# Sixteen unread identity products in TensorE's line ahead of the first inverse

## The chip, the cores and the metric

One Trainium2 chip, one of its cores. The metric is the device time of one launch in microseconds. Between executions of the same kernel it varies: three timed runs of the kernel before gave 660.37, 661.7 and 666.66 us.

## The reference

The inputs are r, k, v, w, a, b of shape (4, 8, 768, 40), that is batch, heads, sequence, head size, and the weights of a gated projection behind it. First a recurrence with a 40 x 40 state for each batch and head:

```python
for t in range(S):
    y[:, :, t] = np.einsum('bhd,bhde->bhe', rt, state)
    Sa = np.einsum('bhde,bhe->bhd', state, at)
    state_decay = state * wt[:, :, None, :] - np.einsum('bhd,bhe->bhde', Sa, bt)
    state = state_decay + np.einsum('bhd,bhe->bhde', vt, kt)
```

Then y, laid out as x of shape (4, 768, 320), goes through the second part:

```python
h = np.maximum(x @ w_in, 0.0)                 # 320 -> 1024
u, v = h[..., :512], h[..., 512:]
v_n = (v - mean(v)) / np.sqrt(var(v) + 1e-06) # over the last axis
v_s = np.einsum('ts,bsd->btd', w_spatial, v_n) + b_spatial[None, :, None]
return (u * v_s) @ w_out                      # 512 -> 320
```

## The kernel before

`tile_kernel` (line 36) runs `phase1` (217), which does the recurrence and the first product up to u and the normalised v, and then `phase2` (102), which does the product over time, the gate and the last product.

**Chunks and steps.** The recurrence is taken in chunks of C = 64 tokens: 12 chunks for each of two pairs of batches, together NS = 24 steps. A step handles 16 batch-and-head states at once: NU = 8 units, each with two heads on the two halves of the 128 partitions. Within a chunk the sequential rule becomes linear algebra: products of the decayed inputs, a triangular system that is solved with an inverse of 64 x 64 blocks, and an update of the state Mc that the next step reads.

**The inversion.** Four steps (GS = 4) share one inversion. `lprime` (325) and `lblock` (340) make the 32 x 32 triangular blocks of a step, `invert` (347) then inverts those of four steps together by forward substitution on VectorE: a transpose into A (351), then 30 pairs of a multiply into the PSUM tile itmp (362) and an add from it (366), each pair on the result of the pair ahead, and two transposes of the result, XT0 (371) and X11 (373). The inversions of the later groups are spread over the steps ahead of their use; the first, `invert(0)`, is issued whole ahead of the steps (line 916), since step 0 needs it.

**Step by step on TensorE.** `c_bp` (526) multiplies the state with the chunk's inputs; `c_ff` (544) takes the block products; `b_zt` (467) and `b_x21` (494) finish the 64 x 64 inverse from XT0 and X11 and the coupling block l21 of `b_l21` (449); `c_xx` (561) applies the inverse; `c_mp` (583) makes the next state, which `c_mp_out` (601, VectorE, line 607) scales; `c_y` (612) and `c_y_out` (623, VectorE, line 631) make the output y. `b_lka` (393), `b_h` (417) and `b_tok` (434, transposes by the identity `ident`) prepare the step behind. ScalarE copies results out of PSUM, GpSimd cuts triangles (`strict`, 404).

**What sets the order.** Each engine has its own line and runs it in order. Within `with tc.manual_schedule()` (863) that order is written by hand: `at(t, fn, ...)` puts a piece of work on a plan, where the whole part of t is the step and the fraction its place in it, and the plan is sorted and issued in that order. Work whose time is 24 or more, and phase 2, is issued outside that block, where a planner with a simulated timeline sets the order. For step 0 these entries bear on the change:

```python
FIRST = dict(REG, tok=0.37, tok_out=0.375, l21=0.45, l21_out=0.452, zt=0.47, zt_out=0.50, x=0.70,
             h=0.80, h_out=0.81, x21=0.65, x21_out=0.71)
at(T["tok"] + dt * par, b_tok, q, par)          # dt = 0.03
at(T["tok_out"] + dt * par, b_tok_out, q, par)
at(0.42, b_zt, 0)
at(0.43, b_xcopy, 0, act_copy)
at(0.44, b_zt_out, 0)
```

So in TensorE's line of step 0 stand `c_bp(0)` (0.00 and 0.05), `b_lka(1)` (0.115), `c_ff(0)` (0.30 and 0.35), `b_tok(1)` (0.37 and 0.40), `b_zt(0)` (0.42), which reads XT0 and so waits for the first inversion, `b_l21(1)` (0.45), `b_x21(0)` (0.455), `b_zt(1)` (0.47) and `c_xx(0)` (0.55 and 0.60).

**PSUM.** Pools ps_k, ps_c, ps_b, ps_i (the tile itmp) and ps_m (the tile pv, 128 x 512, one buffer). pv and itmp are used by the products of x with w_in (`m_ps`, 678; `m_v` 681 with 512 columns, `m_u` 728 with 256), which begin with step 11. Those are fp32r; the products of the recurrence are f32. `ident` is a 128 x 128 f32 identity, made at line 876.

Of the kernel before, what the change touches and what calls it, by code (L numbers as in the profile page):

```python
# [8 lines left out]
F32 = mybir.dt.float32  # L9
# [9 lines left out]
P = 128  # L19
# [12 lines left out]
DH = 512  # L32
# [184 lines left out]
def phase1(ctx, tc, early, late, vtok, win, xs, vns, uts, dscr):  # L217
    nc = tc.nc
# [7 lines left out]
    def pool(name, bufs=1, **kw):  # L226
        return ctx.enter_context(tc.tile_pool(name=name, bufs=bufs, **kw))
# [15 lines left out]
    ps_m = pool("ps_m", 1, space=PSUM)  # L243
# [11 lines left out]
    ident = const.tile([P, P], F32, name="ident")  # L255
# [7 lines left out]
    st, marks = {}, {}  # L263


    def prep_load(s, rows, cols=slice(0, EW), i=None, queues=(nc.sync, nc.sync)):
        t = ein[s % 2 if i is None else i]
        for par in range(2):
            o = par * 64
            queues[par].dma_start(out=t[o:o + rows, cols], in_=early[par, s, 0:rows, cols])  # L270
# [6 lines left out]
    def scan1(s, i=None):  # L277
        t = ein[s % 2 if i is None else i]
        Et = etp.tile([P, WF], F32, name="Et")
        at = fifo[s % 8].tile([P, NU, C], F32, name="at")  # L280
        sl = fifo[s % 8].tile([P, NU, 2, C], F32, name="sl")
        wseg = t[:, 0:WF]
        oth = t[:, WF:].rearrange("p (q n c) -> p n q c", q=3, c=C)
        sx = pin.tile([P, WF], F32, name="S", bufs=2)
        sv = sx.rearrange("p (n c) -> p n c", c=WSEG)
        st["pre", s] = (Et, at, sl)
        st["raw", s] = (wseg, oth, sv)
        nc.vector.tensor_tensor_scan(
            out=sx[:, ::-1], data0=wseg[:, ::-1], data1=ends[:, ::-1],
            initial=0.0, op0=ALU.mult, op1=ALU.add,  # L290
        )
        nc.vector.reciprocal(out=eseg[:, :, 0:1], in_=sv[:, :, 1:2])

    def scan2(s):
        Et, at, sl = st["pre", s]
        wseg, oth, sv = st["raw", s]
        nc.vector.tensor_tensor_scan(
            out=Et, data0=wseg, data1=ends, initial=0.0, op0=ALU.mult, op1=ALU.add,
        )

    def scr_store(s):
        if s % CPB == 0:
            return
        sv = st["raw", s][2]
        sc = jit.tile([P, NU], F32, name="sc")
        nc.scalar.activation(sc, sv[:, :, 1], AF.Copy)
        for par in range(2):
            nc.sync.dma_start(out=scr[s, par], in_=sc[RR[par]])

    def at_mul(s, eng, ns=slice(0, NU)):  # L310
        Et, at, sl = st["pre", s]
        oth = st["raw", s][1]
        Ev = Et.rearrange("p (n c) -> p n c", c=WSEG)
        eng.tensor_tensor(out=at[:, ns], in0=oth[:, ns, 0], in1=Ev[:, ns, 0:C], op=ALU.mult)

    def sl_mul(s, eng, ns=slice(0, NU)):
        Et, at, sl = st["pre", s]
        wseg, oth, sv = st["raw", s]
        k = ns.stop - ns.start
        eng.tensor_tensor(  # L320
            out=sl[:, ns], in0=oth[:, ns, 1:],
            in1=sv[:, ns, 2:C + 2].unsqueeze(2).broadcast_to([P, k, 2, C]), op=ALU.mult,
        )

    def lprime(s, units=range(NU)):
        Et, at, sl = st["pre", s]
        if units[0] == 0:
            st["pl", s] = ps_k.tile([P, NU, HB], F32, name="bk")
        pl = st["pl", s]
        for n in units:  # L330
            for blk in range(2):
                for par in range(2):
                    o = (1 - par) * 64 + blk * HB
                    cs = slice(blk * HB, (blk + 1) * HB)
                    nc.tensor.matmul(  # L335
                        pl[o:o + HB, n, :], lhsT=sl[PR[par], n, par, cs], rhs=at[PR[par], n, cs],
                        start=True, stop=True,
                    )

    def lblock(s):  # L340
        if s % GS == 0:
            st["Lc", s // GS] = inv.tile([P, GS * NU, HB], F32, name="Lc")
        Lc = st["Lc", s // GS]
        u0 = (s % GS) * NU
        nc.scalar.activation(Lc[:, u0:u0 + NU, :], st.pop(("pl", s)), AF.Copy, scale=-1.0)
# [33 lines left out]
    def lin_load(s, par):  # L379
        nc.sync.dma_start(out=lin[s % 2][RR[par], :, 0:LATE], in_=late[par, s])  # L380

    def vtok_load(s, par):
        nc.sync.dma_start(out=Rts[s % 2][par][PR[1 - par], :, C:], in_=vtok[s, par])
# [26 lines left out]
    def b_lka_out(s, par):  # L410
        At = st["blk", s][0]
        pk = st["pk", s]
        ev = PR[1 - par]
        nc.scalar.activation(At[par][ev], pk[ev], AF.Copy)  # L414
        strict(At[par][ev], NU)
# [97 lines left out]
    def grp(g):  # L513
        return slice(g * NP, (g + 1) * NP), range(g * NP, (g + 1) * NP)
# [229 lines left out]
    def at(t, fn, *args):  # L744
        plan.append((t, len(plan), fn, args))

    def step(gen):
        next(gen, None)

    v, p = nc.vector, nc.gpsimd  # L750

    def act_copy(out, in_):
# [4 lines left out]


    M1, M2, M3, M4 = 0.22, 0.46, 0.65, 0.80
    for s in range(NS):  # L760
        at(s + 0.02, scn_load, s)
        for g in range(NB):
            at(s + 0.00 + 0.05 * g, c_bp, s, g)
            at(s + 0.04 + 0.05 * g, c_bp_out, s, g)
            at(s + 0.30 + 0.05 * g, c_ff, s, g)
            at(s + 0.34 + 0.05 * g, c_ff_out, s, g)
            at(s + 0.55 + 0.05 * g, c_xx, s, g)
            at(s + 0.60 + 0.05 * g, c_xx_out, s, g)
            at(s + 0.74 + 0.02 * g, c_mp, s, g)
            at(s + 0.755 + 0.02 * g, c_mp_out, s, g)  # L770
            at(s + 0.86 + 0.04 * g, c_y, s, g)
            at(s + 0.90 + 0.04 * g, c_y_out, s, g)
            at(s + 0.95 + 0.01 * g, y_store, s, g)
# [34 lines left out]
    for q in range(GS, NS):  # L808
        t = PREP.get(q, q - 8 + 0.01)
# [47 lines left out]
    def pads(eng, t):  # L857
        w = t[:, 0:WF].rearrange("p (n c) -> p n c", c=WSEG)
        eng.memset(w[:, :, 1:C + 1], 1.0)
        eng.memset(w[:, :, 0:C + 2:C + 1], 0.0)  # L860
        eng.memset(t[:, WF:], 0.0)

    with tc.manual_schedule():
        W, O = slice(0, WF), slice(WF, EW)
        qs = (nc.sync, nc.scalar)
        nc.vector.memset(eseg[:, :, 0:C + 1], 0.0)
        nc.vector.memset(eseg[:, :, C + 1:], 1.0)
        pads(v, ein[1])
        pads(p, ein[2])
        pads(p, ein[3])  # L870
        for q, cols in ((0, W), (1, W), (0, O), (1, O), (2, W), (2, O), (3, W), (3, O)):
            prep_load(q, 48 if q else 64, cols, q, qs)
        for par in range(2):
            lin_load(0, par)
            vtok_load(0, par)
        make_identity(nc, ident)
        for t in (Mc, *xfs):
            p.memset(t, 0.0)
        for q in range(2):
            for rows in RR:  # L880
                diag = ident[rows, rows.start:rows.start + E]
                nc.scalar.activation(
                    lin[q][rows, :, LATE:], diag.unsqueeze(1).broadcast_to([E, NU, E]), AF.Copy
                )
        for q in range(2):
            scan1(q, q)
            scan2(q)
        for q in range(GS):
            if q > 1:
                scan1(q, q)  # L890
                scan2(q)
            scr_store(q)
            at_mul(q, v)
            for h in range(2):
                sl_mul(q, v, grp(h)[0])
                lprime(q, grp(h)[1])
            if q:
                lblock(q - 1)
        lblock(GS - 1)
        for par in range(2):  # L900
            b_copy(0, par)
        prep_load(4, 48)
        b_lka(0)
        for par in range(2):
            b_lka_out(0, par)
            b_tok(0, par)
            b_tok_out(0, par)
        b_l21(0)
        b_l21_out(0)
        b_h(0)  # L910
        for par in range(2):
            b_h_out(0, par)
            lin_load(1, par)
            vtok_load(1, par)
        prep_load(5, 48)
        for _ in invert(0):
            pass
        open_fifo()
        st["dec"] = late_bufs.enter_context(tc.tile_pool(name="dec", bufs=1))
# [3 lines that stand above are left out]
        at(0.455, b_x21, 0)  # L923
        at(0.46, b_x21_out, 0)
        plan.sort()
        n = 0
        while plan[n][0] < NS:
            t, _, fn, args = plan[n]
            fn(*args)
            n += 1  # L930
# [58 lines left out]
```

## Time and profile before

| | |
|---|---|
| timed runs, median (lowest to highest) | 661.7 us (660.37 to 666.66) |
| profiled execution, its own time | 664.58 us |
| its span, first to last instruction | 662.9 us |
| mean granted TensorE clock over the span | 0.941 |
| busy: TensorE, its weight loads, VectorE, ScalarE, GpSimd | 577.4, 523.0, 445.2, 394.3, 225.2 us |
| matmuls | 10960 |

The profile is of one execution on the chip. A row of a timeline has the start and length of a group of like instructions in us from the start of the span, the engine (PE is TensorE, PEld its weight loads, DVE VectorE, ACT ScalarE, POOL GpSimd), the line of the kernel, the operation, the tiles written and read, their shapes and the count; in brackets stands the idle time of the engine ahead of the group and what ended it. "Issue" is time in which an engine waited for nothing that the profile shows. The granted clock is the share of full speed that the throttle gave TensorE; in this profile it is either 1.0 or 0.5, and a figure between is a mean over a stretch. Matmuls are pipelined: the length of one is its own start to end, and the steps from start to start are shorter.

### The profile page before, as it was taken

What the parts mean: (1) busy time and instruction counts of PE and PEld (TensorE: products, weight loads), DVE (VectorE), ACT (ScalarE), POOL (GpSimd) and SP (SyncE); (2) the same over time, 40 slices, a digit from 0 to 9 for tenths busy, and PEclk for the clock granted to TensorE, in tenths of its full rate; (3) what the DMA queues carried; (4) which work ended last, traced back from release to release, by engine and by line L of the source; (5) the groups of instructions that cost most, each with busy time, mean ns of one, the idle gap of its engine ahead of it and who ended that gap; (6) DMA issues with size and microseconds to landing.
All of it is one profiled execution on the core that took longest, in us unless ns stands there. A gap on an engine that the chain in (4) does not pass through costs nothing.

```text
span 662.9 us, 25888 instructions
## 1 busy us (share of the span) xinstructions
PE 577.4 (87%) x10960; PEld 523.0 (79%) x10960; DVE 445.2 (67%) x951; ACT 394.3 (59%) x884; POOL 225.2 (34%) x312
## 2 busy tenths in 40 slices
PE   1628876478788888999999999999999999999998
PEld 1527766367677777888888888888888999999997
DVE  8898559978999999689787666443375844322221
ACT  2226654358676777788878888888774643232112
POOL 3113213104323334352341342323344935352121
PEclk9977787869798889999999999999999999999999
DMA  8754866458574756656666356365386558150001
GB/s 201 125 101 65 137 140 128 91 123 137 125 160 120 147 111 141 133 141 147 158 179 179 82 144 172 83 168 164 100 238 196 170 165 250 49 169 31 31 30 60
DMA packets 106587, 87.68 MB, mean 132 GB/s; under 512 B 35752, under 2 KB 92328, under 8 KB 104552
## 3 DMA queue, kind: packets, MB, share of 16 engines
q1 hardware_dynamic: 105928, 84.31, 52.4%
q10 hardware_dynamic: 544, 1.72, 1.1%
q8 instruction: 86, 1.41, 1.0%
q14 instruction: 29, 0.24, 0.1%
HBM read 59.20 MB, written 20.50 MB: 120 GB/s over the span
## 4 chain that ended last, share of the span: by engine, by line
PE 67%; DVE 13%; issue 7%; ACT 5%; DMA 5%; SPq 2%; POOL 1%; DVEq 0%; ACTq 0%; POOLq 0%
PE po L199 6%; PE pv L736 6%; PE pv L689 6%; PE pg L179 5%; PE pg L181 5%; PE pg L180 5%; PE bp L532 5%; PE ch L550 4%; PE ch L568 4%; PE bk L422 3%; PE bk L438 3%; DVE itmp L362 3%; PE bk L398 3%; DMA ein<-in_early 3%; DVE A L366 2%
## 5 line engine op out<-in xcount | busy, mean ns | idle before, releaser
L405 POOL TENSOR_SCALAR_AFFINE_SELECT Rt<-Rt 64x512 f32<-64x512 f32 (+1 forms) x144 | 83.8, 583 | 149.1 <-ACT Rt L578 113.6
L405 POOL TENSOR_SCALAR_AFFINE_SELECT At<-At 64x512 f32<-64x512 f32 x48 | 40.3, 840 | 149.9 <-ACT At L414 137.5
L362 DVE TENSOR_TENSOR itmp<-A 128x30 f32<-128x30 f32 (+9 forms) x180 | 68.7, 382 | 3.5
L542 ACT ACTIVATE Rt<-bp 64x416 f32<-64x416 f32 x96 | 49.1, 512 | 35.0 <-PE bp L532 33.2
L179 PE MATMUL pg<-wsh,vh 128*128 128x384 f32 x192 | 64.5, 336 | 1.1 <-ACT vh L51 1.1
L183 DVE TENSOR_TENSOR g<-pg,bb 128x384 f32<-128x384 f32 x32 | 17.8, 556 | 70.6 <-PE pg L181 67.9
L180 PE MATMUL pg<-wsl,vh 128*128 128x384 f32 x192 | 64.4, 335 | 0.0
L366 DVE TENSOR_TENSOR A<-A,itmp 128x30 f32<-128x30 f32 (+9 forms) x180 | 59.1, 328 | 6.1
L181 PE MATMUL pg<-wsh,vl 128*128 128x384 f32 x192 | 63.1, 336 | 0.0
L532 PE MATMUL bp<-lin,Mc 40*64 40x104 f32 x768 | 47.7, 280 | 16.7 <-DVE y L631 14.2
L532 PEld LDWEIGHTS bp<-lin,Mc 40*64 40x64 f32 x768 | 40.9, 151 | 20.2 <-DVE y L631 17.1
L55 POOL TENSOR_TENSOR gl<-g,gh 128x384 fp32r<-128x384 f32 x32 | 33.7, 1056 | 57.5 <-ACT gh L51 57.5
L578 ACT ACTIVATE Rt<-ch 64x416 f32<-64x416 f32 x96 | 49.2, 512 | 5.1 <-PE ch L568 2.7
L550 PE MATMUL ch<-Rt,At 128*64 128x104 f32 x768 | 46.9, 281 | 3.4 <-issue 2.6
L51 ACT ACTIVATE gh<-g 128x384 fp32r<-128x384 f32 x32 | 16.7, 522 | 54.5 <-DVE g L184 54.5
L550 PEld LDWEIGHTS ch<-Rt,At 128*64 128x64 f32 x768 | 41.3, 155 | 7.5 <-issue 4.2
L335 PE MATMUL bk<-at,sl 64*32 64x32 f32 x1536 | 22.4, 208 | 28.1 <-DVE sl L320 15.9
L335 PEld LDWEIGHTS bk<-at,sl 64*32 64x32 f32 x1536 | 18.7, 119 | 31.4 <-issue 13.2
L568 PE MATMUL ch<-ffs,xf 64*64 64x104 f32 x768 | 43.2, 267 | 0.0
L55 POOL TENSOR_TENSOR vl<-raw,vh 128x512 fp32r<-128x512 f32 x24 | 31.7, 1333 | 29.4 <-ACT vh L51 27.3
L607 DVE TENSOR_TENSOR Mc<-ch,scn 104x160 f32<-104x160 f32 x44 | 18.6, 439 | 32.8 <-PE ch L596 26.2
L568 PEld LDWEIGHTS ch<-ffs,xf 64*64 64x64 f32 x768 | 38.3, 144 | 1.1
(128 smaller groups left out, 1508.7 us busy)
## 6 DMA issues: line engine op xcount, KB each, us to landing
ein<-in_early SPq DMA_DIRECT2D x108, 129.0 KB
lin<-in_late SPq DMA_DIRECT2D x48, 160.0 KB
At<-at SPq DMA_DIRECT2D x48, 128.0 KB
uts<-ur SPq DMA_DIRECT2D x48, 128.0 KB
vns<-vr SPq DMA_DIRECT2D x24, 256.0 KB
raw<-vns SPq DMA_DIRECT2D x24, 256.0 KB
ut<-uts SPq DMA_DIRECT2D x24, 256.0 KB
Rt<-in_vtok SPq DMA_DIRECT2D x48, 80.0 KB
```

The lines of the kernel that those rows point to most:

```text
L55: eng.tensor_tensor(out=lo, in0=x, in1=hi.bitcast(F32), op=ALU.subtract)
L179: nc.tensor.matmul(pg, lhsT=vh[:, dc], rhs=w_h, start=(i == 0), stop=False)
L180: nc.tensor.matmul(pg, lhsT=vh[:, dc], rhs=w_l, start=False, stop=False)
L181: nc.tensor.matmul(pg, lhsT=vl[:, dc], rhs=w_h, start=False, stop=(i == NT - 1))
L362: nc.vector.tensor_tensor(out=tp, in0=A[:, k + 1:, k:k + 1].broadcast_to([P, m, k]), in1=A[:, k:k + 1, 0:k].broadcast_to([P, m, k]), op=AL ...
L366: nc.vector.tensor_tensor(out=A[:, k + 1:, 0:k], in0=A[:, k + 1:, 0:k], in1=tp, op=ALU.add)
L405: nc.gpsimd.affine_select(out=t, in_=t, pattern=[[0, k], [1, C]], base=0, channel_multiplier=-1, compare_op=ALU.is_gt, fill=0.0,)
L532: nc.tensor.matmul(bp[PR[par], q, :], lhsT=Mc[RR[par], n, :], rhs=li[RR[par], n, C:], start=(q == 0), stop=False, skip_group_check=True,)
L542: nc.scalar.activation(Rt[par][PR[par], gp, :], st["bp", g][PR[par]], AF.Copy)
L550: nc.tensor.matmul(ff[PR[1 - par], q, :], lhsT=At[par][:, n, :], rhs=Rt[par][:, n, :], start=True, stop=True,)
L568: nc.tensor.matmul(xx[ev, q, :], lhsT=xf[ev, n, :], rhs=ffs[ev, q, :], start=True, stop=True,)
L578: done = nc.scalar.activation(Rt[par][PR[par], gp], xx[PR[1 - par]], AF.Copy, scale=-1.0)
```

## The change

A helper `beat(k)` issues k matmuls of the identity by itself: the stationary operand is `ident`, the moving one `ident` repeated four times (512 columns), the target a PSUM tile pv that is allocated from ps_m ahead of the hand-written block. Each starts and ends its own accumulation. Sixteen of them are put on the plan at 0.415 of step 0. Nothing reads what they write.

```diff
     def step(gen):
         next(gen, None)
 
+    def beat(k):
+        for _ in range(k):
+            nc.tensor.matmul(
+                st["beat"], lhsT=ident, rhs=ident.unsqueeze(1).broadcast_to([P, 4, P]), start=True, stop=True
+            )
+
     v, p = nc.vector, nc.gpsimd
...
     M1, M2, M3, M4 = 0.22, 0.46, 0.65, 0.80
+    for t, k in [(0.415, 16)]:
+        at(t, beat, k)
     for s in range(NS):
...
+    st["beat"] = ps_m.tile([P, DH], F32, name="pv")
     with tc.manual_schedule():
```

## The prediction

> **What bounds the kernel now, at the place of the change.** I read the page first (span 662.9 us, TensorE busy 87% of it), then TensorE's timeline around step 0, then VectorE's over the same stretch, then the granted clock by windows. TensorE's timeline (start, duration, both in us; in brackets the idle time before a group and what ended it):
>
> ```profile
> 36.93 1.09 PE L438 MATMUL bk<-ident,sl 128*128 128x128 f32 x8
> 52.17 1.06 PE L474 MATMUL bk<-XT,l 32*32 32x32 f32 x32 [14.15 <-DVE XT L371]
> 54.16 1.06 PE L501 MATMUL bk<-zt,X 32*32 32x32 f32 x32
> 56.15 3.04 PE L568 MATMUL ch<-ffs,xf 64*64 64x104 f32 x32
> 65.25 1.64 PE L532 MATMUL bp<-lin,Mc 40*64 40x104 f32 x32
> ```
>
> The last thing TensorE does ahead of its long wait is the pair of b_tok(1) transposes, done at 36.93 + 1.09 = 38.02. The next instruction in its line, the first product of b_zt(0), waits 14.15 us for the transposed inverse and starts at 52.17. VectorE, which makes that inverse, shows no gap in the stretch:
>
> ```profile
> 50.12 1.91 DVE L371 STREAM_TRANSPOSE XT<-A 128x1024 f32<-128x1024 f32 x1
> 51.88 1.99 DVE L373 STREAM_TRANSPOSE X<-A 128x1024 f32<-128x1024 f32 x1
> 61.74 0.78 DVE L607 TENSOR_TENSOR Mc<-ch,scn 104x160 f32<-104x160 f32 x2
> 63.58 0.41 DVE L631 TENSOR_TENSOR y<-bp,Et 104x256 f32<-104x256 f32 x1
> 64.67 0.42 DVE L631 TENSOR_TENSOR y<-bp,Et 104x256 f32<-104x256 f32 x1 [0.67 <-PE bp L618]
> 95.16 1.95 DVE L351 STREAM_TRANSPOSE A<-Lc 128x1024 f32<-128x1024 f32 x1 [5.23 <-ACT Lc L345]
> ```
>
> So the end of the wait is set by VectorE alone (50.12 + 1.91 = 52.03), and after it VectorE runs on without a wait until 63.99; TensorE first holds it up at 64.67, for 0.67 us. At 95.16 VectorE waits 5.23 us for the input of the second inversion, which hangs on TensorE's pace in steps 1 and 2: a gain that TensorE still has there would go on. The second thing that lies in the wait is the clock. The columns of these rows are the stretch, its length, busy us (and count) of PE, PEld, DVE, ACT and POOL, then the granted clock, the DMA share and GB/s:
>
> ```profile
> 40.00:42.00 2.00, 0.00 (x0) 0.00 (x0) 1.86 (x5) 0.00 (x0) 0.00 (x0) 1.00 0.72 152
> 42.00:44.00 2.00, 0.00 (x0) 0.00 (x0) 1.83 (x6) 0.00 (x0) 0.00 (x0) 0.60 0.32 71
> 50.00:52.00 2.00, 0.00 (x0) 0.00 (x0) 1.97 (x3) 0.00 (x0) 0.00 (x0) 0.50 0.00 0
> 52.00:54.00 2.00, 1.83 (x64) 1.79 (x64) 2.00 (x3) 1.85 (x5) 0.00 (x0) 0.50 0.03 8
> 58.00:60.00 2.00, 2.00 (x48) 1.71 (x46) 1.93 (x4) 1.61 (x4) 1.51 (x2) 0.63 0.34 87
> 60.00:62.00 2.00, 2.00 (x55) 1.41 (x54) 1.97 (x3) 1.94 (x7) 1.93 (x2) 1.00 1.11 145
> ```
>
> The clock is full when TensorE stops at 38.02. A mean of 0.60 in 42 to 44 means that it was full for (0.60 - 0.50) / 0.50 x 2 = 0.4 us of that window: it fell to half at 42.4, 4.4 us after the last matmul. It came back at 60 - (0.63 - 0.50) / 0.50 x 2 = 59.5. So the 7.3 us of work from 52.17 to 59.5 ran at half clock, and only this could the change improve: its sixteen products compute nothing that is used.
>
> **The change part by part.** Removed: nothing. Moved: nothing; no DMA, no vector, scalar or GpSimd instruction changes place. Added: one allocation of the PSUM tile pv ahead of the steps, and sixteen matmuls of the 128x128 identity with itself repeated four times (512 columns, f32) at 0.415 of step 0, that is behind b_tok(1) and its copies (0.37 to 0.405) and ahead of b_zt(0) (0.42). They wait for nothing that is late: the identity is long written (b_tok reads it), and no one else has touched pv. The next user of pv is the product phase that starts with step 11; it is on TensorE too, so the order alone keeps it behind. They start at 38.02.
>
> Cost of one. No product of this shape is in the trace; the nearest are these (rows of duration give ns min/median/max; the pv row is from the chain, with start and length):
>
> ```profile
> L438 PE MATMUL bk<-ident,sl x8: 272/273/329, 36.9 to 37.7; 128*128 128x128 f32 x8
> L438 PE MATMUL bk<-ident,sl x8: 421/421/472, 94.6 to 96.1; 128*128 128x128 f32 x8
> 94.59 1.97 PE L438 MATMUL bk<-ident,sl 128*128 128x128 f32 x8
> 77.26 2.94 PE L568 MATMUL ch<-ffs,xf 64*64 64x104 f32 x32
> 97.32 1.64 PE L568 MATMUL ch<-ffs,xf 64*64 64x104 f32 x32
> 301.39 2.04 PE pv L689 x8
> ```
>
> Eight f32 transposes of 128 columns took 1.09 us at full clock, the last of them 0.27 from its own start to its end, so seven steps took 0.82: 0.117 us per 128 columns, 0.47 for 512. At half clock the same sum is (1.97 - 0.42) / 7 = 0.221, which halved gives 0.111 and 0.44 for 512. The half-array f32 products of L568 stand beside them: 32 in 1.64 us; if two share the array, that is 16 pairs at 0.1025 per 104 columns, or 0.50 for 512, start and drain included. The lower end is the 512-column fp32r product, 2.04 / 8 = 0.255. The upper end is a full-array f32 product that costs both halves of such a pair one after the other: 2 x 0.50 = 1.01 at full clock. I take 0.45, by the transposes, since they fill the array as the new products do and have the identity as an operand. Sixteen take 7.2 us at full clock and end at 38.02 + 7.2 = 45.2 (bounds 4.1 and 16.2 us: 42.1 and 54.2). At half clock, were it granted, 0.90 each makes 14.4 us and 52.4, or 0.2 us into the work; that is the most which the likely product can cost.
>
> What hides them is VectorE's inversion until 52.03: 14.15 us of cover for 7.2 us. Without that cover they would cost their 7.2 us. Their gain: the clock. Put 4.4 us behind 45.2, the fall comes at 49.6, and b_zt(0) at 52.17 finds half clock as before. TensorE then has the same small products in the same order, so the clock returns where it did, and nothing after 52.17 moves. The sum is 0.
>
> [...]
>
> The profiled execution took 664.58 us, its span 662.9 and 1.68 around it; with a sum of 0 the same execution would again take 664.58. It lies 2.9 above the median of the three timed runs (661.7; 660.37 to 666.66), so the forecast for the median is 661.7. A difference of about 1%, 6.6 us, is what a measurement of this kernel can tell from none.
>
> **The rivals.** [...]
>
> *The products slow the inversion (the other side).* Each step of the inversion writes and reads the PSUM tile itmp on VectorE while the new products write 512 columns each to PSUM. The rows show what a neighbour can do:
>
> ```profile
> 31.27 0.34 DVE L362 TENSOR_TENSOR itmp<-A 128x168 f32<-128x168 f32 x1
> 36.29 0.56 DVE L362 TENSOR_TENSOR itmp<-A 128x234 f32<-128x234 f32 x1
> 38.21 0.42 DVE L362 TENSOR_TENSOR itmp<-A 128x240 f32<-128x240 f32 x1
> 40.87 0.41 DVE L362 TENSOR_TENSOR itmp<-A 128x234 f32<-128x234 f32 x1
> 44.70 0.36 DVE L366 TENSOR_TENSOR A<-A,itmp 128x198 f32<-128x198 f32 x1
> 45.87 0.34 DVE L362 TENSOR_TENSOR itmp<-A 128x168 f32<-128x168 f32 x1
> ...
> 35.94 1.42 POOL L405 TENSOR_SCALAR_AFFINE_SELECT At<-At 64x512 f32<-64x512 f32 x2 [2.11 <-ACT At L414]
> ```
>
> At 36.29, with GpSimd at work (35.94 to 37.36), the 234-element step took 0.56 in place of the 0.41 of its twin at 40.87. Sixteen steps lie beside the products (38.21 to 44.70); at 0.15 each they would delay 52.03 by 2.4 us, and all behind it: 661.7 + 2.4 = 664.1. It decides from the first step that is longer, since VectorE has no slack before 52.03. Against it: at 31.27 TensorE was as busy, writing PSUM, and the step took the same 0.34 as at 45.87, when TensorE stood still.
>
> *The products overrun the wait.* From 0.88 us each (14.15 / 16) the wait ends on TensorE. [...] Only at half clock and the upper end together, 2 x 2.94 / 16 / 104 x 512 = 1.81 each, do they cost 38.02 + 29.0 - 52.17 = 14.8 us, and 676.5. The rows at 36.93 rule out the half clock at their start.
>
> *Code loading shifts.* TensorE has waits that nothing in the profile explains ("issue"), and its instructions come by DMA:
>
> ```profile
> PE bk L335 <- issue: 8.7, 6, 2.1
> PE ch L550 <- issue: 2.6, 1, 2.6
> PE bp L532 <- issue: 2.0, 1, 2.0
> PE bk L398 <- issue: 1.6, 1, 1.6
> ...
> q8 instruction: 86, 1.41, 1.0%
> ```
>
> 1.41 MB in 86 packets is 16.4 KB each, and 25888 instructions in 1.41 MB are 54 bytes each. The change adds 32 (a load and a product, sixteen times), 1.7 KB, a tenth of a packet, so each later boundary falls some 16 matmuls earlier. If the issue waits lie at such boundaries, some move onto a data wait and vanish, others come out of one; I price this at one of the largest, 2.6 us either way: 659.1 or 664.3.
>
> **How the numbers follow.** The forecast (nothing to measure, 661.7) has 0.74; the clock holds 0.08; the inversion is slowed 0.05; code loading shifts 0.11; overrun 0.02. The time is that of the first. The range starts from the lowest run shown less one issue wait, 660.37 - 2.6 = 657.8, which takes in the clock's 1.3, and ends with the highest, 666.7, which takes in the 2.4 and the 2.6. Beyond 1% on the slow side I put 0.04 (the overrun at half clock, and several issue waits that add up), on the fast side 0.03 (issue waits alone), and 0.93 within.
>
> **What would show it.** Right: sixteen products in a block from about 38 to 45.2, then an idle of about 7 us before L474, still released by VectorE's L371 at about 52.0; a granted clock that falls to half between 48 and 52 in place of 42.4, and is half in the 2 us behind 52; L474 at 1.06 and L568 near 3.0 again; inversion steps of unchanged length. [...] Wrong on the cover: L371 later than 50.4, or L474 waiting for nothing. The forecast as a whole is wrong if the median moves by over 1%; then the issue waits and the order of the last phase, which isn't written by hand, come first.

## The result and the profile after

The changed kernel took 666.4 us in the median of 20 runs (661.19 to 673.58), the kernel before 661.55 (657.1 to 667.63): a ratio of 1.0066, with a 95% interval of 1.004 to 1.0092. The forecast was no difference and 661.7; the time lies just inside the range, but the kernel is slower, by an amount that is small and clear of noise. The ratios leave out executions over 1.5% above the fastest of their kernel (three of these 20), so a median and its ratio can differ by some tenths of a per cent.

One execution varies by more than the effect. The profiled one of the changed kernel took 661.19 us, the lowest of its 20; that of before 664.58, above its median. The two spans can't be set against each other as they stand; single stages can, with other profiles beside them.

```profile
span 659.5 us, 25953 instructions
PE 585.3 (89%) x10992; PEld 523.1 (79%) x10992; DVE 439.5 (67%) x951; ACT 393.2 (60%) x884; POOL 223.4 (34%) x312
```

The page has 10992 matmuls in place of 10960: 32 more, not 16. TensorE's timeline of the changed kernel around the place (start, length, in brackets the idle time ahead):

```profile
35.43 13.90 PE L752 MATMUL pv<-ident 128*128 128x512 f32 x32
52.12 0.69 PE L474 MATMUL bk<-XT,l 32*32 32x32 f32 x32 [2.79 <-DVE XT L371]
54.03 0.81 PE L501 MATMUL bk<-zt,X 32*32 32x32 f32 x32 [0.60 <-ACT zt L483]
55.81 3.04 PE L568 MATMUL ch<-ffs,xf 64*64 64x104 f32 x32
67.45 1.67 PE L532 MATMUL bp<-lin,Mc 40*64 40x104 f32 x26
```

Each product of the code is two matmuls on the chip, and the block takes 13.90 us, 0.87 a product, not 0.45. It ends at 49.33, 2.79 us ahead of the inverse. The clock by windows (stretch, length, busy us of PE, PEld, DVE, ACT, POOL, then the granted clock, DMA share, GB/s):

```profile
40.00:42.00 2.00, 2.00 (x6) 0.89 (x5) 1.86 (x5) 0.00 (x0) 0.00 (x0) 1.00 0.70 173
50.00:52.00 2.00, 0.00 (x0) 0.00 (x0) 1.97 (x3) 0.00 (x0) 0.00 (x0) 1.00 0.00 0
54.00:56.00 2.00, 1.97 (x66) 1.79 (x68) 1.93 (x3) 1.50 (x5) 0.00 (x0) 0.61 0.00 0
58.00:60.00 2.00, 2.00 (x44) 1.67 (x44) 1.93 (x4) 1.59 (x5) 1.78 (x3) 0.50 0.36 99
66.00:68.00 2.00, 1.93 (x79) 1.78 (x77) 1.59 (x2) 0.38 (x1) 0.58 (x1) 0.50 0.61 136
68.00:70.00 2.00, 2.00 (x63) 1.93 (x59) 1.90 (x4) 1.24 (x3) 0.00 (x0) 0.98 1.06 140
```

The block holds the clock full over the inversion, L474 (`b_zt`) runs in 0.69, and then the clock falls at 54.4, with TensorE at work, and is back only at 68.0. L568 takes its 3.04 as before. VectorE in the changed kernel:

```profile
40.81 0.41 DVE L362 TENSOR_TENSOR itmp<-A 128x234 f32<-128x234 f32 x1
50.06 1.91 DVE L371 STREAM_TRANSPOSE XT<-A 128x1024 f32<-128x1024 f32 x1
65.56 0.42 DVE L631 TENSOR_TENSOR y<-bp,Et 104x256 f32<-104x256 f32 x1 [1.26 <-PE bp L618]
66.41 0.42 DVE L631 TENSOR_TENSOR y<-bp,Et 104x256 f32<-104x256 f32 x1 [0.43 <-PE bp L618]
```

The inversion isn't touched: the 234-element step beside the block takes 0.41 as before, and L371 starts at 50.06 against 50.12. In this execution L532 (`c_bp` of step 1) starts 2.2 us later than in that of before; yet the execution is the shortest of the twenty, so a late step 0 alone doesn't make one long.

**Two things that step 0 doesn't show.** First, the order of the two programs. Set side by side from the two traces, the engines' lines are the same but for the sixteen products (and for small products that overlap and start almost together) until late. In the changed kernel SyncE, which issues DMAs, has six of them in another order at 339 to 347 us and more from 401 on; VectorE's order is another from 437, ScalarE's from 478, TensorE's from 498, where the last products with w_in and phase 2 stand among each other, and GpSimd's from 515. Second, TensorE's waits that nothing explains stand at other work. Before, and then in the changed kernel, between 60 and 108 us:

```profile
68.51 1.15 PE L398 MATMUL bk<-at,sl 64*64 64x64 f32 x32 [1.62 <-issue]
74.45 0.22 PE L335 MATMUL bk<-at,sl 64*32 64x32 f32 x2 [1.02 <-issue]
86.35 0.65 PE L335 MATMUL bk<-at,sl 64*32 64x32 f32 x52 [1.21 <-issue]
92.45 1.20 PE L550 MATMUL ch<-Rt,At 128*64 128x104 f32 x21 [2.57 <-issue]
105.55 0.26 PE L335 MATMUL bk<-at,sl 64*32 64x32 f32 x7 [1.26 <-issue]
```

```profile
72.66 0.47 PE L335 MATMUL bk<-at,sl 64*32 64x32 f32 x34 [0.47 <-issue]
82.49 0.76 PE L618 MATMUL bp<-Rt,tk 128*40 128x64 f32 x19 [0.98 <-issue]
86.86 0.80 PE L398 MATMUL bk<-at,sl 64*64 64x64 f32 x20 [1.30 <-issue]
101.07 0.54 PE L335 MATMUL bk<-at,sl 64*32 64x32 f32 x39 [1.79 <-issue]
```

Counted from the start of TensorE's records (loads, products and the rest), every such wait over 0.25 us, in both kernels, stands at a number that leaves 193 on division by 256. So the waits stand 256 records or a multiple of it apart. And ahead of each a packet of 16384 bytes is on the instruction queue; for the first, from 65.29 to 66.96, and in both kernels one has landed 1.2 to 2.3 us before the wait ends. I take it from this that TensorE's code comes in pieces of 256 instructions, one packet each, and call the place where two meet a boundary; at 16384 / 256 that makes 64 bytes an instruction, an estimate from these two numbers. The number of packets fits: before, 86 for 22090 records of TensorE (22090 / 256 = 86.3); in the run pad64 below, with 256 instructions more, 87. The waits last up to 2.6 us before and 2.0 in the changed kernel. The change adds 64 instructions, 32 loads and 32 matmuls, a quarter of a piece.

### The profile page after: what moved, and what is told of

Same layout as the page of the kernel before. It is cut to its first block, busy times and chain, and to the rows that moved or that the text cites. A ratio compares the mean times of both kernels' runs of the same rounds, so it can differ in the third digit from the quotient of the medians.

```text
span 659.5 us, 25953 instructions
## 1 busy us (share of the span) xinstructions
PE 585.3 (89%) x10992; PEld 523.1 (79%) x10992; DVE 439.5 (67%) x951; ACT 393.2 (60%) x884; POOL 223.4 (34%) x312
## 4 chain that ended last, share of the span: by engine, by line
PE 65%; DVE 19%; DMA 5%; issue 5%; ACT 4%; SPq 1%; POOL 0%; ACTq 0%; DVEq 0%
PE po L199 6%; PE pv L736 5%; PE pv L689 5%; PE ch L568 5%; PE pg L179 5%; PE pg L180 5%; PE pg L181 5%; PE bp L532 4%; PE ch L550 4%; DVE itmp L362 3%; PE bk L422 3%; DVE A L366 3%; DMA ein<-in_early 2%; PE bp L618 2%; PE bk L438 2%
## 5 line engine op out<-in xcount | busy, mean ns | idle before, releaser
L405 POOL TENSOR_SCALAR_AFFINE_SELECT Rt<-Rt 64x512 f32<-64x512 f32 (+1 forms) x144 | 81.1, 563 | 150.3 <-ACT Rt L578 113.8
L362 DVE TENSOR_TENSOR itmp<-A 128x30 f32<-128x30 f32 (+9 forms) x180 | 66.2, 368 | 3.5
L179 PE MATMUL pg<-wsh,vh 128*128 128x384 f32 x192 | 64.5, 336 | 1.7 <-ACT vh L51 1.7
L532 PE MATMUL bp<-lin,Mc 40*64 40x104 f32 x768 | 48.4, 282 | 12.7 <-DVE y L631 11.8
L532 PEld LDWEIGHTS bp<-lin,Mc 40*64 40x64 f32 x768 | 41.7, 153 | 16.1 <-DVE y L631 14.8
L51 ACT ACTIVATE gh<-g 128x384 fp32r<-128x384 f32 x32 | 16.7, 520 | 54.4 <-DVE g L184 54.4
L335 PE MATMUL bk<-at,sl 64*32 64x32 f32 x1536 | 21.7, 207 | 26.2 <-DVE sl L320 19.8
L550 PE MATMUL ch<-Rt,At 128*64 128x104 f32 x768 | 44.1, 270 | 0.2
L550 PEld LDWEIGHTS ch<-Rt,At 128*64 128x64 f32 x768 | 38.8, 148 | 4.1 <-issue 1.4
L568 PE MATMUL ch<-ffs,xf 64*64 64x104 f32 x768 | 41.9, 262 | 0.0
L335 PEld LDWEIGHTS bk<-at,sl 64*32 64x32 f32 x1536 | 18.2, 118 | 29.3 <-DVE sl L320 12.9
L568 PEld LDWEIGHTS ch<-ffs,xf 64*64 64x64 f32 x768 | 36.9, 140 | 1.1
```

What stands on the lines that cost most here:

```text
L179: nc.tensor.matmul(pg, lhsT=vh[:, dc], rhs=w_h, start=(i == 0), stop=False)
L362: nc.vector.tensor_tensor(out=tp, in0=A[:, k + 1:, k:k + 1].broadcast_to([P, m, k]), in1=A[:, k:k + 1, 0:k].broadcast_to([P, m, k]), op=AL ...
L405: nc.gpsimd.affine_select(out=t, in_=t, pattern=[[0, k], [1, C]], base=0, channel_multiplier=-1, compare_op=ALU.is_gt, fill=0.0,)
L532: nc.tensor.matmul(bp[PR[par], q, :], lhsT=Mc[RR[par], n, :], rhs=li[RR[par], n, C:], start=(q == 0), stop=False, skip_group_check=True,)
L550: nc.tensor.matmul(ff[PR[1 - par], q, :], lhsT=At[par][:, n, :], rhs=Rt[par][:, n, :], start=True, stop=True,)
L568: nc.tensor.matmul(xx[ev, q, :], lhsT=xf[ev, n, :], rhs=ffs[ev, q, :], start=True, stop=True,)
```

## The experiments

Four theories. **C**: the granted clock, which now falls inside step 0, costs. **T**: the planner's other order in the last part costs. **L**: code loading costs by where the boundaries fall. **P**: added TensorE work in the gap costs by itself. Since the planner's order can be read off the program, variants were chosen by it: some have the block and the order of before, some the order of the changed kernel and no block. What the runs measured, all against the kernel before on the same chip:

| run | block | added instructions | order | ratio (95%) |
|---|---|---|---|---|
| again16 | 13.9 us | 64 | changed | 1.0098 (1.0067 to 1.013) |
| block496 | 13.5 | 64 | before | 1.0074 (1.0036 to 1.0112) |
| short7 | 6.2 | 28 | changed | 1.0072 (1.0037 to 1.0107) |
| onecol16 | none | 64 | before | 1.0037 (1.0001 to 1.0074) |
| alloc_only | none | 0 | before | 1.0001 (0.9966 to 1.0036) |
| pad64 | none | 256 | before | 1.0007 (0.9976 to 1.0039) |
| early16 | none | 64 | before | 1.0068 (1.0038 to 1.0097) |
| block14_pad50 | 12.2 | 256 | before | 1.0015 (0.998 to 1.005) |
| changed_pad48 | 13.9 | 256 | changed | 1.0034 (1.0003 to 1.0065) |
| early64 | none | 256 | changed | 1.0057 (1.003 to 1.0083) |
| block496_pad48 | 13.5 | 256 | before | 0.9994 (0.9961 to 1.0027) |
| early32 | none | 128 | before | 1.0016 (0.9987 to 1.0046) |
| early16b | none | 64 | before | 1.0049 (1.0023 to 1.0075) |
| early8 | none | 32 | before | 0.9997 (0.9962 to 1.0033) |
| early24 | none | 96 | before | 1.0086 (1.0048 to 1.0123) |
| early48 | none | 192 | before | 1.0061 (1.0033 to 1.0088) |

"Order before" or "changed" is for TensorE in the last part; for block496, block14_pad50 and block496_pad48 SyncE's line differs a little from that of before, and short7 differs a little from the changed kernel on SyncE, and early64 on SyncE, VectorE and ScalarE.

**The changed kernel again, and its parts apart.** Expected of again16:

> The changed kernel unaltered, so that the others have it beside them. All theories: as in the result, 0.7% above the kernel before (some 4 us). Its profile shows whether the half-clock stretch behind 52 us is again long (about 13 us).

It came out at 1.0098. In its profile the clock stayed full from the block until 67.0, and step 0 shows what that brings:

```profile
38.37 13.90 PE L752 MATMUL pv<-ident 128*128 128x512 f32 x32
55.87 1.85 PE L568 MATMUL ch<-ffs,xf 64*64 64x104 f32 x32
```

The last product of c_y in step 0 ended at 63.3, against 64.6 before and 66.4 in the first profile of the changed kernel: the same program, 1.3 us to the good or 1.8 to the bad by the execution. But L532 behind it started at 65.46 in again16, no earlier than the 65.25 of before, since it then waited for VectorE's y; and the run with the good step 0 was slow all the same.

```diff
-                st["beat"], lhsT=ident, rhs=ident.unsqueeze(1).broadcast_to([P, 4, P]), start=True, stop=True
+                st["beat"].rearrange("p (r c) -> p r c", r=4)[:, :, 0:124], lhsT=ident, rhs=ident.unsqueeze(1).broadcast_to([P, 4, P])[:, :, 0:124], start=True, stop=True
```

> Sixteen products of 496 columns in place of 512: the block lasts about 13.4 us in place of 13.9 and holds the clock over the inversion as before, with the same 64 added instructions, but on TensorE, VectorE, ScalarE and GpSimd the planner's order of the last part is that of the kernel before. Theory T (the loss is the planner's other order in the last part): back to the kernel before, within 0.2%. Theory C (the loss is the clock, which now falls inside step 0): 0.7% slower, as the changed kernel. Theory L (the 64 added instructions shift code loading): 0.7% slower too.

Slower by 0.74%: T alone falls as the whole cause.

```diff
-    for t, k in [(0.415, 16)]:
+    for t, k in [(0.415, 7)]:
```

> Seven products of 512 columns: a block of about 6 us, after which the clock falls ahead of 52 us as without them; but the planner's order of the last part is the changed kernel's on TensorE, VectorE, ScalarE and GpSimd. T: 0.7% slower than before. C: equal to before, within 0.2%. L: something between, as 28 instructions are added and not 64.

Slower by 0.72%, with a block that ended at 41.8 and a clock that fell at 44.9: against C alone. The 28 instructions do little by themselves (32 alone, below, made 0.9997), so most of this is likely the order.

```diff
-                st["beat"], lhsT=ident, rhs=ident.unsqueeze(1).broadcast_to([P, 4, P]), start=True, stop=True
+                st["beat"][:, 0:1], lhsT=ident, rhs=ident[:, 0:1], start=True, stop=True
```

> Sixteen products with one column each: the same 64 added instructions, some 4 us of weight loads and next to no products, the planner's order as before. T and C: equal to before, within 0.2%. L: 0.7% slower.

Slower by 0.37%, a smaller figure than L asked for; its median lies 0.89% higher (668.4 against 662.53). With neither block nor other order it stands against both C and T as the only cause.

**The boundary put back.** A small product was added for these, `pad(k)`, placed at 0.416 of step 0 or, in the runs named early, and in the two named pad48, right behind `make_identity(nc, ident)`, where TensorE has nothing to do yet:

```diff
+    def pad(k):
+        for _ in range(k):
+            nc.tensor.matmul(
+                st["beat"][0:32, 0:1], lhsT=ident[:, 0:32], rhs=ident[:, 0:1], start=True, stop=True
+            )
```

First the control, `(0.415, 0)` in the plan:

> The allocation of pv alone, with no product. All theories: equal to the kernel before, within 0.2%. A difference here would mean that the comparison itself is off by as much.

1.0001. Then pad(64) in place of the sixteen products:

> In place of the sixteen products sixty-four small ones (32 columns of the identity, one moving column): as two loads and two products each on the chip, 256 instructions of 64 bytes, one whole code packet of 16 KB, so that every later packet boundary falls at the same work as before; next to no activity for the clock, the planner's order as before. Theory L (code loading by where the boundaries fall): equal to before, within 0.2%. A theory P (any added TensorE work in the gap costs, whatever the boundaries): 0.4 to 1% slower. C (clock) and T (planner): equal to before.

1.0007: with a whole piece of 256 added, four times the instructions of the changed kernel, nothing is lost, and P falls. Its unexplained waits are back at the work of before:

```profile
68.50 1.70 PE L398 MATMUL bk<-at,sl 64*64 64x64 f32 x32 [1.56 <-issue]
74.44 0.22 PE L335 MATMUL bk<-at,sl 64*32 64x32 f32 x2 [0.97 <-issue]
85.38 0.65 PE L335 MATMUL bk<-at,sl 64*32 64x32 f32 x52 [1.59 <-issue]
90.12 1.20 PE L550 MATMUL ch<-Rt,At 128*64 128x104 f32 x21 [1.20 <-issue]
...
104.70 0.26 PE L335 MATMUL bk<-at,sl 64*32 64x32 f32 x7 [2.74 <-issue]
```

The counts tell it: x32, x2, x52, x21 and x7 are those of before, to the single matmul. The 64 instructions alone, far from step 0 (`pad(16)` early, no block):

> Sixteen small products right behind the making of the identity, ahead of TensorE's first real work, where it stands idle to 11.8 us: 64 instructions as in the changed kernel, none of them in the gap of step 0. L: 0.4 to 1% slower, as the boundaries fall 64 instructions earlier all the same. P, C and T: equal to before, within 0.2%.

Slower by 0.68%: L holds without any work in the gap. It was run once more:

> The run with sixteen small early products once more. L: again 0.4 to 1% slower, steps 12 to 22 again 198 us or more against 197, and the part behind step 22 some 187 against 186.

1.0049, and the waits of that profile are at the work that the changed kernel's were, x19 of L618, x19 of L398 (x20 there) and x39 of L335:

```profile
68.16 1.37 PE L532 MATMUL bp<-lin,Mc 40*64 40x104 f32 x26 [2.35 <-issue]
74.22 0.47 PE L335 MATMUL bk<-at,sl 64*32 64x32 f32 x33 [1.62 <-issue]
84.06 0.76 PE L618 MATMUL bp<-Rt,tk 128*40 128x64 f32 x19 [0.99 <-issue]
89.81 0.80 PE L398 MATMUL bk<-at,sl 64*64 64x64 f32 x19 [2.62 <-issue]
103.99 0.54 PE L335 MATMUL bk<-at,sl 64*32 64x32 f32 x39 [0.97 <-issue]
```

Its step figures were as expected: 198.9 us from the end of step 11 to that of step 22, 186.7 behind it.

**The block alone.** Fourteen products and pad(50) at 0.416; then the 496-column block with pad(48) early:

> Fourteen products of 512 columns (12.2 us) and fifty small ones behind them: the clock is held over the inversion as in the changed kernel, but 256 instructions are added, one whole code packet, and the planner's order is that of before on TensorE, VectorE, ScalarE and GpSimd. L: equal to before or up to 0.2% faster. C (the clock that falls inside step 0 costs): 0.4 to 1% slower. T: equal to before.

> The sixteen products with 496 columns, 256 added instructions in all by forty-eight small ones ahead of the first work, the planner's order that of before on four engines. Only the block itself and its clock remain. L and T: equal to before. C: slower by 0.3% or more; if the held clock gains, up to 0.2% faster.

1.0015 and 0.9994: with the boundaries and TensorE's order put back, the block costs or gains at most the 0.5% that the intervals leave. In their two profiles the clock was not held as expected; it fell just ahead of the inverse, at 51.3 us until 68.4 in block14_pad50 and at 51.5 until 58.4 in block496_pad48. That makes step 0 of block14_pad50 as late as that of the changed kernel (67.88 against 67.45, where L532 starts), and the time is still that of before:

```profile
67.88 1.32 PE L532 MATMUL bp<-lin,Mc 40*64 40x104 f32 x20
```

So C falls. The clock over whole executions speaks against it too: in the 20 runs of the changed kernel its mean is 0.951, in the kernel before, in the experiments' rounds, 0.941 to 0.943. The slower kernel has the fuller clock.

**The planner's order alone.** pad(64) early, no block; and the whole changed kernel with pad(48) early:

> Sixty-four small products ahead of TensorE's first work and none in step 0: 256 instructions, one code packet; no block, so the clock is as before; but the planner's order of the last part is on TensorE that of the changed kernel. L alone: equal to before. T: 0.4 to 0.7% slower, all of it behind step 22.

> The changed kernel whole, with the planner's order of the last part exactly its own, and forty-eight small products ahead of TensorE's first work: 192 more instructions, 256 with the change's 64, one code packet. Only the code shift is undone. L alone (the shift is the whole loss): equal to before, within 0.2%. L and T together (the planner's other order costs some 4 us in the last part, as the profiles so far suggest): 0.4 to 0.7% slower.

1.0057 and 1.0034: T holds as a second cause, with early64's order not quite that of the changed kernel. TensorE's waits from 470 us on, before, then in the changed kernel, then in early64 (in total, times, longest):

```profile
PE pv L736 <- ACT vr L691: 1.3, 1, 1.3
PE pg L179 <- ACT vh L51: 1.1, 1, 1.1
```

```profile
PE pv L736 <- ACT ur L738: 3.3, 2, 3.1
PE pg L179 <- ACT vh L51: 1.7, 1, 1.7
PE pv L736 <- ACT vr L691: 1.2, 1, 1.2
```

```profile
PE pg L179 <- ACT vh L51: 2.0, 1, 2.0
PE pv L736 <- ACT vr L691: 1.2, 1, 1.2
PE ch L568 <- ACT ffs L558: 0.6, 1, 0.6
PE pv L736 <- ACT ur L738: 0.4, 1, 0.4
```

In the changed kernel TensorE waits 3.3 us, which it didn't wait before, for ScalarE to empty the single PSUM buffer pv (3.4 in again16, 1.6 in changed_pad48, 2.0 in short7). TensorE's own order is still that of before at this place; it is ScalarE's that is another. Before, then in the changed kernel:

```profile
482.30 0.39 ACT L738 ACTIVATE ur<-pv 128x256 f32<-128x256 f32 x1
483.75 0.85 ACT L51 ACTIVATE xh<-xt 128x768 fp32r<-128x768 f32 x1 [0.41 <-DMA xt<-xs]
```

```profile
477.68 0.84 ACT L51 ACTIVATE xh<-xt 128x768 fp32r<-128x768 f32 x1 [2.96 <-DMA xt<-xs]
478.55 0.38 ACT L738 ACTIVATE ur<-pv 128x256 f32<-128x256 f32 x1
```

The planner has put the conversion of x (`xh`), whose input comes by DMA, ahead of the copy that empties pv. ScalarE stands 2.96 us for the DMA, and the copy and TensorE behind it stand too. In early64 `xh` comes one copy later, so pv is emptied in time; there the wait of L179 for ScalarE is 2.0 in place of 1.1.

**The shift as a curve.** pad(8), pad(24), pad(32) and pad(48) early:

> Eight small early products, 32 instructions. L: a time between that of no shift and that of 64, so 0 to 0.7% slower; whichever it is, the boundaries in the trace fall 32 instructions earlier in the work.

> Twenty-four small early products, 96 instructions. L: between the shifts of 64 (0.7% slower) and 128 (0.2% slower).

> Thirty-two small products ahead of TensorE's first work: 128 instructions, half a code packet; the planner's order as before. L: another time than before, on either side, since every boundary falls on other work (I expect 0.3 to 1% slower). T, C: equal to before.

> Forty-eight small early products, 192 instructions. L: not known in advance, since it depends on what work the boundaries meet; if the shift is a curve with the period of 256, some value within 1% of before, faster or slower. If the added TensorE work itself were the cause, slower than the run with sixteen, by over 0.7%.

By added instructions: 0 1.0001, 32 0.9997, 64 1.0068 and 1.0049 (with other products in place of the small ones 1.0074 in block496 and 1.0037 in onecol16), 96 1.0086, 128 1.0016, 192 1.0061, 256 1.0007. The two runs at 32 and 128 were no slower within their intervals, where 0.3 to 1% was expected of 128, and 96 lay above 64 and not between 64 and 128 as expected. More added work doesn't cost more; where the boundaries fall does. No shift was faster than none, so no version beat the kernel before.

**In which stage.** Step ends by the last product of c_y, the rows of step 22 being, before, then in the changed kernel, then in early64 (whose span is 662.0 us):

```profile
476.04 1.09 PE L618 MATMUL bp<-Rt,tk 128*40 128x64 f32 x32
```

```profile
468.50 1.09 PE L618 MATMUL bp<-Rt,tk 128*40 128x64 f32 x32
```

```profile
473.04 1.09 PE L618 MATMUL bp<-Rt,tk 128*40 128x64 f32 x32
```

The part behind it is 662.9 - 477.1 = 185.8 us before, 659.5 - 469.6 = 189.9 in the changed kernel, 662.0 - 474.1 = 187.9 in early64. The same sums for other profiles:

| profiles | end of step 11 | steps 12 to 22 | behind step 22 |
|---|---|---|---|
| order and boundaries of before (before, alloc_only, pad64, block14_pad50, block496_pad48) | 272.8 to 280.2 | 196.9 to 197.5 | 185.7 to 186.5 |
| 64 shifted, order of before (early16, early16b, block496) | 280.1 to 281.2 | 198.0 to 199.0 | 186.7 to 187.3 |
| 256, order changed (early64, changed_pad48) | 276.9 and 276.0 | 197.2 and 198.2 | 187.9 and 188.9 |
| 64 shifted, order changed (the changed kernel, again16) | 271.7 and 278.0 | 197.9 and 197.2 | 189.9 and 190.0 |

So the other order costs 2 to 3 us behind step 22, and with the shift 4. The shift costs 1 to 2 us in steps 12 to 22 and about 1 behind them with the order of before.

In steps 12 to 22 the loss can be traced to the waits. TensorE's unexplained waits in this stage are none before and in pad64; in block496, one of the second row, they are these (in total, times, longest):

```profile
PE bp L532 <- issue: 1.0, 1, 1.0
PE bk L501 <- issue: 0.5, 1, 0.5
PE bk L335 <- issue: 0.3, 1, 0.3
```

Over the profiles the stage lasts 196.9 to 197.1 us where they are none (before, pad64, early48), 199.0 with 1.6 (early16b) and with 1.9 (block496), and 200.0 with 2.8 (early24); the others follow to within half a microsecond, at about 1.1 us for each 1 us of wait, but for early32, whose clock fell in this stage. Behind step 22 no profile has such a wait, so the 1 us that the shift seems to cost there isn't explained by it. What the order costs there is TensorE's idle time: 2.3 us in all before, 4.2 in early64, 5.3 in changed_pad48, 6.3 in the changed kernel.

Ahead of step 12 single profiles scatter by 10 us: the three of the second row lie 4 us above the five of the first in the mean, the two of the last row don't, and what the shift costs there stays open. Left out of the table are early8, early24 and short7, whose clock fell once at about 500 us, for 3 to 7 us, onecol16, whose profiled execution (671.3 us) was one of its longest, and early32 and early48, whose boundaries are others again.

## Why the prediction was wrong

**Right:** what bounds the place (VectorE's inversion, 50.06 against 50.12), the cover of the block, that the inversion would not slow, and that the block by itself changes the time by nothing that can be measured (1.0015 and 0.9994). The 1.3 us that the range takes in for the clock is shown by no run: in again16, with the clock full until 67.0, L532 started at 65.46 against 65.25, and counted from the start of L474 after 12.92 us in place of 13.08. The last product of c_y did end 64.6 - 63.3 = 1.3 earlier there, but L532 behind it waited for VectorE's y.

**Wrong, without effect: the cost of one product.** The step was "if two share the array, that is 16 pairs". The row of L568 has 32 matmuls; but the code issues 16 products there (4 units, two halves, two groups), so each of these f32 products is two matmuls, and the 32 are 8 pairs of products, not 16. The transposes, which I took the value from, are one matmul each (8 in the code, 8 in the row), and so about half as dear per column (0.47 us for 512 by my sum, against 0.87). The stated upper end, 1.01, was near the truth, 13.90 / 16 = 0.87; I had the count of the code to check it with. The clock was full when the work behind the inverse began, at 52.12, where the forecast had it at half and gave 0.08 to a clock that holds. But it didn't hold either: it fell at 54.4, with TensorE at work since 52.12, and stayed half for 13.7 us, 13.5 of them with TensorE busy. In again16, where the block ended 0.27 us ahead of L474 and not 2.79, it held until 67.0 and was half for 3.4. From the end of TensorE's last product, or of the block, to the fall it was 4.4 us before, 3.1 in short7 (44.9 - 41.8) and 5.1 in the changed kernel (54.4 - 49.3), there 2.3 us into the work behind the inverse; so no run shows the 4.4 us as a fixed delay, nor the 48 to 52 that the forecast gave for the fall. What decides it isn't shown. That "the clock returns where it did" was wrong as well: 68.0 against 59.5.

**Wrong, and the reason: the sum of 0.** The step that failed is "nothing after 52.17 moves", and with it "Moved: nothing; no DMA, no vector, scalar or GpSimd instruction changes place". Two things move that are in no engine's row of step 0. One is the code's boundaries, which show in where the unexplained waits stand. The prediction had the mechanism as a rival, but it halved the instructions (32 for 64), put 54 bytes to each where 16384 bytes for 256 records make 64 (it divided the bytes of one queue by the instructions of all engines), priced it at one wait "either way" and gave it 0.11; measured, 64 instructions alone cost 0.68% and 0.49%, 4.5 and 3.2 us. I had read a symmetric chance where nothing said that it was one. The other is the order of the last part, which the prediction named in its last sentence and gave no price: with the boundaries put back it is 0.34% (changed_pad48, the order exactly) to 0.57% (early64), 2.2 to 3.8 us. That the sixteen products would change the planner's order could have been suspected from the code, since phase 2 is planned on a simulated timeline that holds them.

**Still open.** The single effects sum to between 0.83% (0.49 and 0.34) and 1.25% (0.68 and 0.57), the changed kernel measures 0.66% and, again, 0.98%; the intervals allow a sum that is less than full, and don't settle it. That the waits at the boundaries are late code is argued from their places and the packets ahead of them, and shown only as far as moving the boundaries moves the waits and the time. Of the 3 to 4.5 us that the shift costs, the waits account for the 1 to 2 in steps 12 to 22; where the rest is lost isn't shown.

## What to carry to other kernels

Instructions that are hidden in time were not free here: 64 of them moved TensorE's unexplained waits to other work and cost 0.68% and 0.49% with nothing else changed, 96 cost 0.86%, and 256, the distance that the waits keep, 0.07%, within the noise. Before such an edit is judged, look whether such waits keep a distance, add a padding that brings its size to that, and compare the order of every engine's line, since a planner may have put the rest in another one: here a single conversion ahead of a copy on ScalarE came with 3.3 us of TensorE waiting for that engine. What is left then is the edit (here nothing). Count a row's matmuls against the products in the code before a price is taken from it.

## What the runs showed of the hardware

An f32 product of 128 x 512 by 128 x 128 took 0.87 us at full clock, as two matmuls of 0.434 each (13.90 / 32), while the f32 transposes of b_tok(1) were one matmul each (8 in 1.09 us at full clock). TensorE's unexplained waits over 0.25 us stand 256 records or a multiple of it apart, at the remainder 193 both before (11 waits) and in the changed kernel (13), and last up to 2.6 us before, 2.0 in the changed kernel, 3.1 in block496 and 5.0 in short7. Their sum over the whole program was 16.9 us before and 14.0 in the changed kernel, so it doesn't tell which is slower; within steps 12 to 22 it does. A stretch of half clock over most of step 0 (51.3 to 68.4 us in the profile of block14_pad50, 42.4 to 59.5 before, 7.3 us of it at work) made no difference that 12 runs can tell (block14_pad50: 1.0015, 0.998 to 1.005).
